# A linear-attention recurrence feeding a bilinear FFN: tokens put in order at y's eviction, and a new written-out order of steps

## The chip, the cores and the metric

The kernel runs on one core of a Trainium2 chip. The metric is the device time in microseconds of one execution, as the median of several runs. A core has five engines that run beside each other, each with a queue of its own that it works off in order: TensorE (PE, matmuls; its weight loads are shown as PEld), VectorE (DVE), ScalarE (ACT), GpSimd (POOL) and SyncE (SP, which here only issues transfers). They wait for each other by semaphores. Transfers (DMA) run beside the engines; they are issued from the queues of SP, POOL and, once, ACT.

## The reference

```python
# q, k, v, alpha: (B, H, S, D) = (4, 8, 768, 48), float32
state = np.zeros((B, H, D, D))
for t in range(S):
    state = alpha[:, :, t, :, None] * state + np.einsum('bhd,bhe->bhde', k[:, :, t], v[:, :, t])
    y[:, :, t] = np.einsum('bhd,bhde->bhe', q[:, :, t], state)

x = y.transpose(0, 2, 1, 3).reshape(B * S, H * D)      # 3072 tokens x 384
a = x @ w_a                                            # 384 -> 1536
b = x @ w_b
out = (a * b) @ w_out                                  # 1536 -> 384
```

A state of 48 x 48 for every head and batch row decays by alpha, takes in k v, and is read by q at each of 768 positions. The result is the input of a feed-forward layer without a nonlinearity other than the product a*b.

## The kernel before

**Chunks.** The recurrence is computed in chunks of positions. A chunk c of six holds 2 of the 4 batch rows (each called u, 0 or 1) and 256 positions, so 512 tokens: c // 2 is the stretch of positions, c % 2 the pair of batch rows. Positions lie in pairs: a partition holds two neighbours, r = 0 and 1. Two halves g of 64 pairs make up the 256 positions of a row u. So the columns of y in PSUM for one u and g are 3 x 128 columns (KT = 3 groups of 128 of the 384 features lie on partitions): for each feature group first the 64 positions with r = 0, then the 64 with r = 1. The tokens of an output block of 128 rows must be in their own order, s by s with r inside.

**Steps.** The whole kernel is one string, PROGRAM, of some 850 short steps, each with the number of its chunk; the loop at L1063 to L1068 emits them in that order, which is so the order of every engine's queue. PROGRAM also names the engine of a step where there is a choice (S = ACT, V = DVE, P = POOL, Y = SP) and the PSUM bank (0 to 7) of a step that writes PSUM. The steps that matter here:

- `ld` (L549) loads a, k, q, v from DRAM on SP or POOL; `W`, `Wo` (L527, L531) load weights on POOL.
- `ln`, `ra`, `E`, `l2`, `l2s`, `R`, `H`, `L`, `lv`, `AQ` prepare the decays: logarithms and exponentials on ACT, running sums on PE (`AQ` L633), products on DVE or POOL (`lv` L652). `mq`, `mk` (L678, DVE) multiply q and k by their decays into QKp.
- `C`, `Ce` (L736, L744) turn QKp with PE for chunks 0 and 1. For chunks 2 to 5 `T u` (L767) turns it by a transposing transfer on SP's queue, which writes kqT.
- `dr`, `dl` (L684, L689) write the decay rows to DRAM and bring them back as bl, on SP's queue.
- `K`, `K2` and `k` (L799, L812, L829, L830) update the state: matmuls, then an addition and a multiplication by bl on DVE.
- `D u h t` (L841) makes the scores from kqT; `M` (L846) masks them on DVE, or `Mc` (L850) copies them on ACT and `Mm` (L854) masks the copy on DVE.
- `SB`, `SA`, `Y` (L865) accumulate y of a row u in two PSUM banks, `X u` (L894 to L902) evicts y as bf16 into xT.
- `a f w bank`, `b f w bank` (L919): three matmuls each for 128 of the 1536 hidden features, over 512 tokens (w is `*`) or the 256 of one row u (w is 0 or 1). `as` (L925) copies a to SBUF on ACT, `pr` (L933) multiplies it by b, straight from PSUM, on DVE and writes prod.
- `o m half bank` (L941): six matmuls for a block m of 128 tokens; `ot` (L956 ACT, L958 DVE) evicts it, `st` (L974) stores it on SP. The last block is done in two halves (`oc` L952, `otc`, `stc`).

**Layout of tokens before.** xT is `[128, KT, B, C]`: feature group, then the 4 half-rows, then 128 columns. X copies y as it stands, so that the columns are in the order r, s. A matmul of a or b reads 512 (or 256) adjacent columns of xT as its rhs. The order is put right at pr: the functions `tokens` and `columns` make its output write every second element, r inside s.

Of the kernel before, what the change touches and what calls it, by code (L numbers as in the profile page):

```python
# [17 lines left out]
0: cm 0; c1; cz 0 b P; ci; ld a 0b Y; c1a; ld a 0a Y; ln 0b; cu; cz 1 b P; fill 7 2; cu2 V; cz 0 q V; cus; ld k 0b Y; ld k 0a Y; B 0b 5; ld q 0b Y; ld v 0 P  # L18
0: ln 0a; ld q 0a Y; E 0b b; E 0b i; mq 0b V; B 0a 0; E 0a i; dk 0 2; E 0a b; ld a 1 P; mk 0b V; C 0 1 5; cs 0 m P; ld k 1 P; ld q 1 P; v 0 S; mk 0a V; cm 1
0: de 0; fill 2 1; mq 0a V; C 0 0 3; Ce 0 1 V; W b 0 256; cz 0 v P; Ce 0 0 V; D 0 1 4; ln 1; ld v 1 P; W a 256 768; K 0 0 6; k 0 0 V; M 0 1; D 0 0 0; SB 0 6  # L20
0: cz 1 q P; B 1a 2; M 0 0; W a 0 256; E 1a i; E 1a b; W b 256 768; mq 1a V; mk 1a V; B 1b 4; dk 1 3; E 1b i; E 1b b; de 1; v 1 S; mq 1b V; mk 1b V; C 1 0 0
0: Y 0; SA 0; Ce 1 0 V; cs 1 m P
1: ld a 0 P; ld a 1 P
0: W a 768 1536; C 1 1 1; X 0 S; c2 P; D 1 0 3; W b 768 1536
1: ld q 0 P
0: Ce 1 1 V; K 1 0 5; k 1 0 V; a 4 0 0
1: ld k 0 P
0: D 1 1 6; SB 1 1
1: ld v 0 P; ld q 1 P
0: Mc 1 0; a 3 0 5; Wo 0 6; a 0 0 3; Mm 1 0 V; Mc 1 1; as 0 0; b 0 0 4  # L30
1: ld k 1 P
0: pr 0 0; b 1 0 6; a 2 0 3; a 1 0 7; a 5 0 4; as 2 0; b 2 0 3; Mm 1 1 V; as 1 0; b 4 0 7; as 5 0; b 5 0 4; pr 2 0; pr 1 0
1: ln 0
0: SA 1; Y 1; Wo 6 12; K 1 1 6; as 3 0; as 4 0; X 1 S
1: ra 0
0: K 0 1 3
1: l2 0 V
0: b 3 0 0; pr 5 0; pr 4 0
1: H 0 V; L 0 V
0: a 2 1 1; a 5 1 2; as 5 1; pr 3 0; a 1 1 7; b 4 1 5; b 5 1 4; as 2 1; k 0 1 V; pr 5 1; a 4 1 2; as 1 1  # L40
1: ln 1
0: b 2 1 0; pr 2 1; a 6 * 3; as 4 1; b 1 1 2
1: l2 1 V
0: pr 4 1; as 6 *
1: H 1 V
0: pr 1 1
1: A2 0 7
0: a 11 * 0; a 7 * 5; a 0 1 4
1: L 1 V
0: k 1 1 V  # L50
1: ra 1
0: as 11 *
1: lv 0 q V; E 0 i
0: as 0 1; b 6 * 0; b 11 * 3; a 8 * 4; pr 6 *; pr 11 *
2: ld a * P
0: b 0 1 1; as 8 *; a 3 1 6
1: E 0 b; lv 0 k V
0: a 10 * 2; pr 0 1
1: mq 0 V; ld v 1 P
0: b 8 * 4  # L60
1: A2 1 7
0: as 10 *; b 10 * 2; pr 8 *
1: E 1 b
0: as 3 1; as 7 *; b 9 * 3; b 3 1 0; b 7 * 1; a 9 * 6
2: ld q * P
1: v 0 S; lv 1 q V; mk 0 V
0: pr 10 *
1: mq 1 V; C 0 1 4
0: as 9 *
1: C 0 0 2  # L70
0: o 0 0 5; pr 7 *
1: dk * 6
2: ld k * P
3: ld v * P
0: cz 1 v P; pr 9 *
1: Ce 0 0 S; E 1 i; de *; lv 1 k P; Ce 0 1 V; D 0 1 1; D 0 0 3
0: pr 3 1
1: Mc 0 0; K2 0 0 7 0
0: o 1 0 6
1: mk 1 V; M 0 1  # L80
0: o 3 0 4; o 1 1 -; ot 1 S; c3 P
3: ld a * P
0: cs 1 0 P; o 3 1 -
1: k 0 0 V; k 0 1 V; Mm 0 0 V; SB 0 1; C 1 0 3; C 1 1 7
0: ot 3 S; o 0 1 -
1: Ce 1 0 V
2: ln *
1: v 1 V; D 1 0 3; Ce 1 1 S; K2 1 1 6 0; Y 0; SA 0
0: ot 0 V
1: k 1 0 V; D 1 1 6  # L90
0: o 2 0 5
1: M 1 0
2: l2 0 V
1: X 0 S; a 3 0 1; Mc 1 1
2: l2s 0 P; l2s 1 P
1: a 2 0 3; a 4 0 4
2: R 0
1: k 1 1 V; as 4 0
2: ra 1
1: as 3 0; b 4 0 7  # L100
0: o 2 1 -
1: as 2 0
0: ot 2 S
1: pr 4 0
2: R 1; lv 1 q P
1: b 3 0 6; b 2 0 7; a 5 0 2; pr 3 0; b 5 0 3; as 5 0; b 1 0 5; a 1 0 1; pr 5 0; pr 2 0; a 7 0 2; as 1 0; pr 1 0
2: AQ 3
1: SB 1 6
2: lv 0 k P
1: a 10 0 5  # L110
2: lv 1 k V; ra 0; ld v * P
1: Mm 1 1 V
2: E 1 b
1: as 10 0; b 10 0 0; pr 10 0
2: mq 1 V; E 1 i
1: as 7 0; b 7 0 1
2: E 0 b; E 0 i
1: a 0 0 5
0: st 3 Y
2: dr  # L120
1: SA 1; Y 1
2: mk 1 V
1: pr 7 0; a 11 0 0; a 6 0 3; b 6 0 2; X 1 S; b 11 0 4; a 2 1 6; as 6 0; a 3 1 7; as 11 0; b 2 1 1; pr 6 0
2: lv 0 q V
1: b 4 1 0; as 2 1
2: T 1
1: pr 11 0
2: dl
0: st 0 Y
1: a 0 1 2; pr 2 1  # L130
2: mq 0 V
1: b 3 1 3; b 0 0 6; as 3 1; as 0 0; b 0 1 7; pr 3 1; a 8 0 1; a 9 0 5
0: st 1 Y
1: b 8 0 3; b 9 0 4; pr 0 0; as 0 1
2: mk 0 V
1: a 4 1 2
3: ln *
1: a 9 1 6; pr 0 1; as 8 0; b 9 1 1
3: ra 1
1: b 10 1 7; pr 8 0; a 10 1 3; as 4 1; as 9 0; as 9 1; a 6 1 6; b 6 1 2; b 11 1 5; pr 4 1; as 10 1; pr 9 0; a 11 1 4; pr 10 1; pr 9 1; as 6 1  # L140
2: v 1 S
1: a 8 1 3; b 8 1 1; a 7 1 6; pr 6 1
3: l2 0 V
1: as 11 1
2: T 0
1: as 8 1; a 5 1 4
3: ra 0
1: as 5 1; a 1 1 2
2: v 0 V
4: ld a * Y  # L150
1: pr 11 1; as 7 1; pr 8 1
2: K2 * * 0 7; D 1 1 3; D 1 0 5
1: as 1 1; b 5 1 2; o 2 0 1
2: k * 0 V
1: pr 5 1
3: v 0 S; v 1 S
1: b 1 1 2
2: Mc 1 0; M 1 1
3: l2s 0 P; l2s 1 P
1: b 7 1 0; o 2 1 -; pr 1 1; o 3 0 4  # L160
2: SB 0 5
1: pr 7 1
3: R 0
2: D 0 0 2
1: ot 2 V
2: Mm 1 0 V
1: o 3 1 -
2: Mc 0 0; SB 1 0; D 0 1 2
3: R 1
1: ot 3 S  # L170
2: SA 0
1: o 0 0 4
0: cs 0 0 P
2: Mc 0 1
4: ln *
3: ld q * Y; ld k * Y
2: k * 1 V
3: AQ 2
2: Y 1; SA 1; Mm 0 1 V; Mm 0 0 V; Y 0; X 0 S
3: E 0 b  # L180
4: l2 0 V
2: X 1 V
1: o 0 1 -
2: b 1 * 6; a 1 * 5
3: E 1 b
4: ld k * Y
3: E 1 i
1: ot 0 S
3: E 0 i
4: l2s 0 P  # L190
2: a 0 * 0; b 0 * 1; as 0 *; as 1 *
3: lv 0 k P; lv 0 q P
2: a 5 * 7
1: st 3 Y
2: a 7 * 4
4: l2s 1 P
2: a 2 * 5
3: lv 1 q V; mq 1 V; lv 1 k V
2: pr 1 *
3: dr  # L200
2: pr 0 *
3: mk 0 V
4: ld q * Y
0: st 2 Y
2: as 5 *; a 6 * 6; b 6 * 2; as 7 *
3: mq 0 V
2: b 9 * 4; b 7 * 0
1: st 2 Y
3: dl
4: R 0  # L210
2: b 5 * 7
1: o 1 0 3
2: a 9 * 1; pr 7 *; as 6 *
3: T 0
2: pr 6 *
4: ra 0
2: pr 5 *; a 11 * 6
3: mk 1 V
2: as 9 *; a 3 * 0
4: lv 0 k V; lv 0 q V; R 1  # L220
2: as 2 *
1: o 1 1 -
2: as 11 *; a 8 * 5; b 11 * 2; a 4 * 7; b 2 * 1
3: T 1
1: ot 1 V
2: pr 9 *; as 8 *; pr 11 *; pr 2 *; b 8 * 3; b 4 * 5; as 4 *
5: ld a * Y
3: K2 * * 4 6
2: pr 8 *; as 3 *; pr 4 *
3: k * 0 V; D 0 0 2; Mc 0 0  # L230
2: b 3 * 1
4: ra 1
2: pr 3 *; b 10 * 5; a 10 * 0
3: D 1 0 1; D 1 1 3
2: as 10 *
3: k * 1 V; Mc 1 1
2: o 0 0 7; o 2 0 0
3: M 1 0
5: ln *
2: pr 10 *  # L240
4: lv 1 q P
3: SB 1 3; D 0 1 1; Mc 0 1
4: lv 1 k P
5: ld q * Y
1: st 0 Y
3: SB 0 5
2: o 2 1 -
3: Mm 1 1 V; Mm 0 0 V; Mm 0 1 V
4: ld v * P
2: ot 2 S; o 0 1 -  # L250
4: AQ 0; E 0 b; E 0 i
3: SA 0; Y 0; SA 1
4: E 1 b
3: Y 1
5: l2s 1 V
4: mq 0 V; mk 0 V
3: X 0 S; X 1 S
2: o 3 0 2; o 3 1 -
4: T 0
3: a 5 * 3  # L260
4: E 1 i; v 0 S
3: a 9 * 0
2: ot 3 S
3: b 5 * 6; a 6 * 5; as 5 *
2: st 2 Y
3: as 9 *
5: ld k * P; l2s 0 P
3: as 6 *
5: ra 1
4: mq 1 V  # L270
2: ot 0 S
3: a 0 * 1
4: mk 1 V
3: a 1 * 2
4: D 0 0 3
5: l2 0 V
1: st 1 Y
4: dr
5: R 0
3: pr 5 *  # L280
4: v 1 S; M 0 0
3: b 1 * 7; as 1 *; a 3 * 5; b 9 * 6; pr 9 *; b 6 * 4; a 2 * 0; pr 6 *
4: T 1
5: lv 0 k P
3: b 0 * 6; as 0 *; as 2 *
4: dl
3: a 8 * 1
5: lv 1 q P
3: b 4 * 0; a 4 * 4; b 2 * 3; pr 1 *; pr 0 *; as 8 *; pr 2 *; as 4 *; pr 4 *; b 3 * 6; b 8 * 2
5: ld v * P; lv 1 k P  # L290
3: a 11 * 1
5: ra 0
3: as 3 *; pr 8 *; as 11 *; a 7 * 0
4: D 1 0 3; K * 0 5
5: lv 0 q P
3: pr 3 *; as 7 *
5: v 1 V
4: k * 0 V
5: R 1
4: D 1 1 6; D 0 1 1; Mc 1 0; Mc 1 1; M 0 1  # L300
2: o 1 0 0; o 1 1 -
3: a 10 * 7; b 11 * 3
4: SB 1 4
2: ot 1 S
3: as 10 *
4: Mm 1 0 V
3: pr 11 *
4: SB 0 1
5: AQ 6; E 0 i; E 0 b; mk 0 V
3: b 10 * 0; b 7 * 3  # L310
4: Mm 1 1 V
5: mq 0 V
3: o 2 0 6; pr 7 *
4: Y 0; SA 0
3: pr 10 *
5: E 1 b
4: X 0 V; Y 1; SA 1
2: st 1 Y
3: o 1 0 3
4: X 1 S  # L320
3: o 2 1 -
5: E 1 i
4: a 7 * 2
5: mq 1 V
4: b 7 * 7; a 6 * 1; as 7 *; as 6 *
3: o 1 1 -
4: b 1 * 5; a 0 * 1; a 1 * 4
5: dr; T 0
2: st 3 Y
4: b 6 * 2  # L330
3: ot 2 V
4: pr 7 *; a 5 * 6
5: mk 1 V
3: ot 1 V
4: pr 6 *
5: v 0 S
4: as 0 *; as 1 *; pr 1 *
2: st 0 Y
5: T 1
4: b 0 * 7; as 5 *; pr 0 *; a 4 * 1; a 3 * 0  # L340
5: K * 0 2; dl
4: as 4 *
5: D 1 0 6; D 0 0 3; M 1 0
4: as 3 *
5: D 1 1 0; Mc 1 1; Mc 0 0; k * 0 V
3: o 3 0 5; o 3 1 -; ot 3 S
4: b 4 * 0; a 2 * 2
5: SB 1 3
4: pr 4 *
5: SB 0 6; D 0 1 0; M 0 1  # L350
3: o 0 0 5; o 0 1 -
5: Mm 1 1 V
4: b 5 * 0
3: ot 0 S
4: b 3 * 1
5: Mm 0 0 V
4: pr 5 *; b 10 * 5; a 11 * 0
5: SA 1; Y 1
4: pr 3 *
5: SA 0  # L360
4: as 11 *
5: X 1 S; Y 0
4: as 2 *
5: X 0 V
4: a 10 * 1
3: st 2 Y
4: b 2 * 4; pr 2 *; b 11 * 7; as 10 *; pr 11 *; pr 10 *
3: st 3 Y
4: a 8 * 3
5: b 9 * 2; a 2 * 0; b 4 * 5; a 4 * 1; b 1 * 6  # L370
4: b 8 * 7; as 8 *
5: as 4 *
4: pr 8 *
5: pr 4 *; a 8 * 4; a 1 * 3; as 2 *; as 8 *; b 8 * 0; a 11 * 5; as 1 *
3: st 0 Y
5: b 2 * 4; pr 1 *; pr 8 *; a 3 * 7; pr 2 *; as 11 *; a 5 * 6
4: o 3 0 0; o 1 0 3
5: b 11 * 1
4: a 9 * 4
5: as 5 *; b 5 * 5; as 3 *; pr 11 *; a 9 * 6; b 3 * 7  # L380
4: as 9 *; b 9 * 1
5: a 10 * 4; pr 5 *
# [716 lines left out]
```

## Time and profile before

| what | value |
|---|---|
| median of 3 runs | 194.33 us (194.84, 193.74, 194.33) |
| span of the profiled execution | 192.04 us (page: 192.0) |
| what lies around the span, against the median | 2.3 us |
| PE busy | 186.8 us, 97% |
| PEld busy (beside PE) | 116.9 us |
| DVE busy | 133.1 us, 69% |
| ACT busy | 106.5 us, 55% |
| POOL busy | 56.9 us, 30% |
| granted clock of PE | 9 (90% or more) in all 40 slices |
| DMA | 29.40 MB, mean 153 GB/s |

Busy times of PE are modelled from pipelined matmuls, whose durations overlap: a matmul of 512 columns is listed with 379 ns on average, though the next starts 216 ns later. The starts of neighbouring instructions tell PE's rate. The rows of a group give: line, engine, operation, output<-inputs, tile shape and form, count; then busy us and mean ns of one; then the idle time of the engine before them and what ended it.

### The profile page before, as it was taken

What the parts mean: (1) busy time and instruction counts of PE and PEld (TensorE: products, weight loads), DVE (VectorE), ACT (ScalarE), POOL (GpSimd) and SP (SyncE); (2) the same over time, 40 slices, a digit from 0 to 9 for tenths busy, and PEclk for the clock granted to TensorE, in tenths of its full rate; (3) what the DMA queues carried; (4) which work ended last, traced back from release to release, by engine and by line L of the source; (5) the groups of instructions that cost most, each with busy time, mean ns of one, the idle gap of its engine ahead of it and who ended that gap; (6) DMA issues with size and microseconds to landing.
All of it is one profiled execution on the core that took longest, in us unless ns stands there. A gap on an engine that the chain in (4) does not pass through costs nothing.

```text
span 192.0 us, 6086 instructions
## 1 busy us (share of the span) xinstructions
PE 186.8 (97%) x2613; PEld 116.9 (61%) x2613; DVE 133.1 (69%) x223; ACT 106.5 (55%) x194; POOL 56.9 (30%) x75
## 2 busy tenths in 40 slices
PE   7999999999999999999999999999999999999992
PEld 3888875677778876645557444656465644545562
DVE  2387698994989888899897956887567446252510
ACT  4448885656779867753487756743572435314211
POOL 8999626752450500640074262000000000000000
PEclk9999999999999999999999999999999999999999
DMA  5999999999969999999999989017641200000422
GB/s 132 274 219 218 251 253 235 244 269 264 251 107 166 165 216 265 248 254 149 233 213 181 156 174 129 3 42 140 146 66 44 85 0 0 0 0 3 164 82 82
DMA packets 62618, 29.40 MB, mean 153 GB/s; under 512 B 53712, under 2 KB 60768, under 8 KB 62592
## 3 DMA queue, kind: packets, MB, share of 16 engines
q0 software_dynamic: 18432, 13.37, 39.6%
q1 hardware_dynamic: 44016, 15.55, 38.1%
q8 instruction: 20, 0.33, 0.7%
q10 hardware_dynamic: 144, 0.10, 0.2%
q14 instruction: 6, 0.05, 0.1%
HBM read 25.98 MB, written 4.74 MB: 160 GB/s over the span
## 4 chain that ended last, share of the span: by engine, by line
PE 91%; DMA 5%; SPq 1%; DVE 1%; issue 1%; ACT 0%; DVEq 0%
PE psum L919 47%; PE psum L941 24%; PE psum L865 7%; PE psum L841 3%; DMA kqT<-QKp 3%; DMA q_t<-in_q_dram 3%; PE psum L736 2%; PE psum L633 1%; PE psum L952 1%; SPq L549 1%; PE psum L799 1%; PE psum L812 1%; PE psum L700 1%; PE psum L591 1%; PE psum L592 1%
## 5 line engine op out<-in xcount | busy, mean ns | idle before, releaser
L919 PE MATMUL psum<-xT,wb_t 128*128 128x512 bf16 (+1 forms) x270 | 56.0, 337 | 0.0
L919 PE MATMUL psum<-xT,wa_t 128*128 128x512 bf16 (+1 forms) x270 | 56.0, 337 | 0.0
L941 PE MATMUL psum<-wo_t,prod 128*128 128x384 bf16 x276 | 49.4, 326 | 0.0
L919 PEld LDWEIGHTS <-wb_t 128*128 128x128 bf16 x270 | 25.9, 98 | 19.9 <-issue 0.5
L919 PEld LDWEIGHTS <-wa_t 128*128 128x128 bf16 x270 | 25.9, 98 | 19.7 <-issue 0.3
L941 PEld LDWEIGHTS <-prod 128*128 128x128 bf16 x276 | 25.9, 98 | 17.6
L956 ACT ACTIVATE ot<-psum 128x384 f32<-128x384 f32 (+1 forms) x16 | 7.7, 482 | 22.7 <-PE psum L941 21.6
L850 ACT ACTIVATE m<-psum 128x1024 bf16<-128x1024 f32 x14 | 14.1, 1023 | 4.6 <-PE psum L841 4.3
L613 POOL TENSOR_TENSOR l<-la 64x384 f32<-64x384 f32 x7 | 7.8, 1108 | 26.6 <-ACT la L556 19.0
L846 DVE TENSOR_TENSOR m<-psum,mask 128x1024 bf16<-128x1024 f32 x10 | 12.1, 1220 | 3.1 <-PE psum L841 3.1
L652 POOL TENSOR_TENSOR q_t<-q_t,ra 128x384 f32<-128x384 f32 x5 | 6.1, 1215 | 22.5 <-ACT ra L645 19.7
L556 ACT ACTIVATE la<-a_t 128x1536 f32<-128x1536 f32 (+2 forms) x9 | 9.5, 1055 | 2.3 <-DMA a_t<-in_alpha_dram 2.2
L678 DVE TENSOR_TENSOR QKp<-q_t,beta 128x768 bf16<-128x768 f32 x10 | 10.0, 995 | 1.0 <-ACT beta L667 1.0
L865 PE MATMUL psum<-m,vx 64*64 64x128 bf16 x576 | 10.5, 217 | 0.0
L900 ACT ACTIVATE xT<-psum 128x768 bf16<-128x768 f32 x9 | 7.2, 816 | 5.7 <-PE psum L865 5.5
L678 DVE TENSOR_TENSOR QKp<-k_t,invb 128x768 bf16<-128x768 f32 x10 | 9.7, 972 | 0.8 <-ACT invb L667 0.8
L854 DVE TENSOR_TENSOR m<-m,mask 128x1024 bf16<-128x1024 bf16 x14 | 9.3, 684 | 1.2 <-ACT m L850 1.2
L958 DVE COPY ot<-psum 128x384 f32<-128x384 f32 (+1 forms) x9 | 4.8, 532 | 7.6 <-PE psum L941 4.7
L865 PEld LDWEIGHTS <-vx 64*64 64x64 bf16 x576 | 9.0, 107 | 0.5 <-issue 0.3
L841 PE MATMUL psum<-kqT 64*64 64x128 bf16 x384 | 9.0, 219 | 0.4 <-DMA kqT<-QKp 0.3
L652 POOL TENSOR_TENSOR k_t<-k_t,a_t 128x384 f32<-128x384 f32 x6 | 7.4, 1228 | 6.1 <-issue 3.3
L549 POOL DMA_DIRECT2D v_t<-in_v_dram x8 | 8.5, 1058 | 0.1
(271 smaller groups left out, 287.9 us busy)
## 6 DMA issues: line engine op xcount, KB each, us to landing
out_dram<-ot SPq DMA_DIRECT2D x23, 192.0 KB, 3.8
q_t<-in_q_dram SPq DMA_DIRECT2D x3, 768.0 KB, 6.5
a_t<-in_alpha_dram POOLq DMA_DIRECT2D x2, 768.0 KB, 15.2
k_t<-in_k_dram POOLq DMA_DIRECT2D x2, 768.0 KB, 12.1
v_t<-in_v_dram POOLq DMA_DIRECT2D x4, 384.0 KB, 7.0
a_t<-in_alpha_dram SPq DMA_DIRECT2D x2, 768.0 KB
k_t<-in_k_dram SPq DMA_DIRECT2D x2, 768.0 KB
a_t<-in_alpha_dram POOLq DMA_DIRECT2D x3, 384.0 KB, 8.5
```

Of the source, the lines that this page charges most:

```text
L549: eng.dma_start(out=t[:, us, hs].rearrange("p b h r d -> p (b h) (r d)"), in_=src[ch.b0 + us.start:ch.b0 + us.stop, hs, ch.s * 2 * C:(ch.s ...
L556: nc.scalar.activation(out=ch.la[:, us, hs].rearrange("p b h r d -> p (b h r d)"), in_=ch.a[:, us, hs].rearrange("p b h r d -> p (b h r d) ...
L613: eng.tensor_add(ch.l2[(1 - g) * HC:(2 - g) * HC, 1], x[:, :, 0, :], x[:, :, 1, :])
L652: eng.tensor_mul(x, x, by)
L678: eng.tensor_mul(QKp[ch.c % 2][:, u, j, :, hs, :D], src[:, u, hs].rearrange("p h r d -> p r h d"), f)
L841: nc.tensor.matmul(s2[g * HC:(g + 1) * HC, r, p, rk, :], lhsT=turned_part(ch, u, 1, rk, 2 * h + p, g, rs), rhs=queriesT(ch, u, 2 * h + p, ...
L846: nc.vector.tensor_mul(m.rearrange("p r a k s -> p (r a) (k s)"), ch.s2[u, h].rearrange("p r a k s -> p (r a) (k s)"), maskn(4))
L850: nc.scalar.activation(out=m.rearrange("p r a k s -> p (r a) (k s)"), in_=ch.s2[u, h].rearrange("p r a k s -> p (r a) (k s)"), func=AF.Copy)
L854: eng.tensor_mul(x, x, maskn(4))
L865: nc.tensor.matmul(y[c * DP:(c + 1) * DP, g, j // 2 * C:(j // 2 + 1) * C], lhsT=lhsT, rhs=rhs, start=(g, c) not in begun, stop=False, skip ...
L919: nc.tensor.matmul(p, lhsT=(wa_t, wb_t)[w][:, kk, f * 128:(f + 1) * 128], rhs=ch.xT[:, kk, us, :], start=(kk == 0), stop=(kk == KT - 1))
L941: nc.tensor.matmul(op, lhsT=ch.prod[:, f, at:at + C], rhs=wo_t[:, f, :], start=(f == 0), stop=(f == NFF - 1))
```

## The change

1. xT becomes `[128, B, KT, C]`: half-row, feature group, column. X takes a second argument, g, and evicts one half: 24 steps of 128 x 384 in place of 12 of 128 x 768. Its output is written with r inside s, so every second element of bf16, and the tokens are in their order from there on.
2. The rhs of a and b is `xT[:, us, kk, :]`: four runs of 128 adjacent columns (two for a half), 384 elements apart.
3. pr writes its product as it comes; `tokens` and `columns` are gone. The eviction uses `evict`, which ot uses too.
4. PROGRAM is another order of the same work. It is the same up to `C 1 0`, but for PSUM banks; from there on steps stand elsewhere, and have other banks, engines or forms. Counted over the kernel: PE has the same 2549 matmuls form by form, DVE 236 instructions in place of 223, ACT 193 (and one DMA issue, as before) in place of 194, POOL 78 and SP 61 as before. The loads on POOL's queue stand in the same order among each other.

In the changed kernel line numbers are 48 smaller up to the eviction (846 to 850); a and b are L861, pr L874, evict L897 and L899.

```diff
-    def evac(ch, u, eng):
+    def evac(ch, u, g, eng):
         if not hasattr(ch, "xT"):
-            ch.xT = wk.tile([128, KT, B, C], BF16, name="xT")
-        o_ = ch.xT[:, :, 2 * u:2 * u + 2, :].rearrange("p a g s -> p g a s")
-        i_ = ch.y[u][0][:, :, :KT * C].rearrange("p g (a s) -> p g a s", a=KT)
-        if eng is nc.scalar:
-            nc.scalar.activation(out=o_, in_=i_, func=AF.Copy)
-        else:
-            eng.tensor_copy(o_, i_)
+            ch.xT = wk.tile([128, B, KT, C], BF16, name="xT")
+        evict(ch.xT[:, 2 * u + g].rearrange("p a (s r) -> p a r s", r=2),
+              ch.y[u][0][:, g, :KT * C].rearrange("p (a r s) -> p a r s", a=KT, r=2), eng)
...
-    def tokens(x, us):
-        return x.rearrange("p (b s r) -> p b r s", s=HC, r=2)[:, us]
-
-    def columns(x, n):
-        return x.rearrange("p (b r s) -> p b r s", r=2, s=HC)
-
...
-            nc.tensor.matmul(p, lhsT=(wa_t, wb_t)[w][:, kk, f * 128:(f + 1) * 128], rhs=ch.xT[:, kk, us, :], start=(kk == 0), stop=(kk == KT - 1))
+            nc.tensor.matmul(p, lhsT=(wa_t, wb_t)[w][:, kk, f * 128:(f + 1) * 128], rhs=ch.xT[:, us, kk, :], start=(kk == 0), stop=(kk == KT - 1))
...
-        o_, a_, b_ = tokens(ch.prod[:, f, :], us), columns(a[:, :n], n), columns(b, n)
-        nc.vector.tensor_mul(o_, a_, b_)
+        nc.vector.tensor_mul(ch.prod[:, f, us.start * C:us.stop * C], a[:, :n], b)
...
-        "X": lambda x, u, e: evac(x, int(u), ENG[e]),
+        "X": lambda x, u, g, e: evac(x, int(u), int(g), ENG[e]),
```

Of PROGRAM, three places that the prediction speaks of. After `C 1 0` in chunk 0:

```diff
-0: W a 768 1536; C 1 1 1; X 0 S; c2 P; D 1 0 3; W b 768 1536
+0: W a 768 1536; C 1 1 2; X 0 0 S; X 0 1 S; c2 P; D 1 0 4; W b 768 1536
...
-0: Ce 1 1 V; K 1 0 5; k 1 0 V; a 4 0 0
+0: Ce 1 1 V; K 1 0 0; k 1 0 V; Mc 1 0; K 1 1 3; D 1 1 6; Mc 1 1; b 1 0 2; a 0 0 0; k 1 1 V; a 1 0 1; SB 1 4
```

Chunk 4's transposing transfers (before: T 0, with D 0 0 as the next step on kqT, then T 1):

```diff
-4: T 0
-3: a 5 * 3
-4: E 1 i; v 0 S
...
-4: D 0 0 3
...
-4: T 1
-5: lv 0 k P
-3: b 0 * 6; as 0 *; as 2 *
-4: dl
+4: v 1 S; mk 0 V; T 0
+3: Y 1; X 1 0 V
...
+4: T 1
+2: ot 0 S
+3: as 9 *; as 8 *
+5: lv 1 q P
+4: dl
+3: b 8 * 0; pr 8 *; as 1 *; b 1 * 2
...
+4: D 1 1 0
...
+4: D 0 1 4; D 0 0 6; v 0 V; M 0 0; M 0 1
```

Chunk 5's:

```diff
-5: dr; T 0
...
-5: mk 1 V
...
-5: T 1
-4: b 0 * 7; as 5 *; pr 0 *; a 4 * 1; a 3 * 0
-5: K * 0 2; dl
-4: as 4 *
-5: D 1 0 6; D 0 0 3; M 1 0
-4: as 3 *
-5: D 1 1 0; Mc 1 1; Mc 0 0; k * 0 V
...
+5: lv 0 q P; mq 0 V; T 0; v 1 V
+4: Y 0; X 0 1 S; Mm 1 0 V; Mm 1 1 V; Y 1
+3: pr 5 *; o 0 0 0; o 2 0 3; o 1 0 5
+5: mq 1 V; mk 1 V; T 1
+4: X 1 1 V; X 0 0 V; X 1 0 S; a 7 * 4
+3: pr 10 *; pr 7 *; o 0 1 -; o 1 1 -; ot 1 V
+5: D 0 0 6
+4: as 7 *
+3: ot 0 S
+5: Mc 0 0; dl; K * 0 2; k * 0 V; D 0 1 0; M 0 1; D 1 1 4; Mc 1 1
+3: o 2 1 -; ot 2 S
+4: a 4 * 2; as 4 *; b 7 * 4; pr 7 *
+3: o 3 0 0
+5: SB 1 2; SB 0 4; D 1 0 6; Mm 0 0 V; M 1 0
```

## Prediction

> **What bounds the kernel now.** I read the page's busy shares first, then the chain that ended last, then the chain's pieces in order of time, then the groups of instructions with shapes kept apart, and last SP's queue around chunk 5.
>
> The page, parts 1, 2 and 4:
>
> ```profile
> span 192.0 us, 6086 instructions
> PE 186.8 (97%) x2613; PEld 116.9 (61%) x2613; DVE 133.1 (69%) x223; ACT 106.5 (55%) x194; POOL 56.9 (30%) x75
> ...
> PE   7999999999999999999999999999999999999992
> ...
> PEclk9999999999999999999999999999999999999999
> ...
> PE 91%; DMA 5%; SPq 1%; DVE 1%; issue 1%; ACT 0%; DVEq 0%
> ```
>
> TensorE is busy in every slice between the first and the last, at the full granted clock. A busy PE need not be PE at its rate, so the chain's pieces decide (start, length, what):
>
> ```profile
> 106.47 4.99 DMA kqT<-QKp
> 111.50 0.42 PE psum L841 x16
> 111.92 9.17 PE psum L919 x42
> ...
> 129.08 1.80 PE psum L865 x120
> ...
> 141.65 0.68 PE psum L841 x46
> ...
> 152.81 11.11 PE psum L919 x51
> ...
> 188.69 0.33 ACT ot L956
> ```
>
> 9.17 us for 42 matmuls of L919 and 11.11 for 51 are 218 ns for 512 columns: they run back to back. In the single instructions the starts lie 216 ns apart at 512 columns, 109 at 256, 163 at 384 (L941), and each change between 128x128 and 64x64 tiles and back costs about 0.3 us. The sum of these over all of PE's instructions is 185.3 us. Outside the first 12 us, where little can be fed to PE, I find only two waits: 0.14 us at 24.4 and 0.36 us at 111.1, the end of the transfer that the first line shows (T of chunk 4, issued at 106.47). The last matmul ends at 188.65; an eviction, a store's issue and its landing fill the rest up to 192.04. So the time is PE's work, plus a start and a tail of a few us each, plus 0.5 us of waits. A change can win no more than these waits if it leaves PE's work alone. It can lose by a slower matmul, or by making PE wait.
>
> The span is 192.04; the median is 194.33, so 2.3 us lie around the span, and I add them at the end. The three runs lie 0.3% to either side of the median; 0.5%, or 0.97 us, is about what a measurement of this kernel can tell from no change.
>
> **The parts of the change, and their cost.** The groups, shapes apart (mean ns of one is after the busy time):
>
> ```profile
> L941 PE MATMUL psum<-wo_t,prod 128*128 128x384 bf16 x276 | 49.4, 326 | 0.0
> L919 PE MATMUL psum<-xT,wa_t 128*128 128x512 bf16 x162 | 41.2, 379 | 0.0
> L865 PE MATMUL psum<-m,vx 64*64 64x128 bf16 x576 | 10.5, 217 | 0.0
> L841 PE MATMUL psum<-kqT 64*64 64x128 bf16 x384 | 9.0, 219 | 0.4 <-DMA kqT<-QKp 0.3
> L900 ACT ACTIVATE xT<-psum 128x768 bf16<-128x768 f32 x9 | 7.2, 816 | 5.7 <-PE psum L865 5.5
> L958 DVE COPY ot<-psum 128x384 f32<-128x384 f32 x8 | 4.4, 554 | 4.7 <-PE psum L941 4.7
> ```
>
> *PE's instructions.* Both kernels have the same matmuls, form by form (540 of a and b, 276 of o, 24 of oc and the rest). Only the order differs, which changes tile sizes 57 times in place of 56: +0.3 us.
>
> *The rhs of a and b.* It was 512 adjacent bf16; now it is four runs of 128, 384 elements apart (two runs at half width). No row has this shape, so I bound it. From below: L841 reads its rhs as two runs of 64, and 46 such matmuls took 0.68 us, 14.8 ns each (four run at once on the quarters of the array); L865 reads one run of 128 from m, and 120 took 1.80 us, 15.0 ns each. Breaks between runs cost nothing there. Below nothing is excluded, since 216 ns is what the contiguous form takes and the columns stay as many. From above: L633, whose rhs takes every second element, starts its 384 columns 183 ns apart where L941 needs 163; 20 ns on each of 540 matmuls would be 10.8 us. The new rhs is of L841's kind, with longer runs; I take 0.
>
> The Trainium skill speaks against this edit: "Advanced Engine Details and Errata", section "Memory Cachelines", asks for at least two hits on a 16-byte line of SBUF for full rate, and under "PSUM Cachelines" says that any non-contiguous access pattern significantly slows matmuls. By its first rule, runs of 256 bytes hit each line eight times and the sum gets 0, as with L841; by the second, read for SBUF too, the sum would end as in the second rival below. The rows of L841 and L865 bear out the first reading.
>
> *The eviction X.* 12 of 768 columns (816 ns on ACT, 952 on DVE) become 24 of 384, written with a stride of two elements. Nearest rows: 384-wide evictions, 492 ns on ACT and 554 on DVE (L958). Strided bf16 writes cost pr about 8% per element against other DVE rows, so 500 to 600 ns is the bound. A pair costs some 0.2 us more than one X did, on both engines together about 2.4 us over the kernel; but the first half is done 0.3 us sooner. Both engines have room (69% and 55% busy), and between SB/SA/Y and the first a of a chunk, matmuls of the chunk before fill PE. On the path: 0.
>
> *pr.* Its write is now contiguous. Before: 54 of about 725 ns and 36 of 441. At the per-element rate of L829 and L846 it would be about 690 and 424: 54 x 35 + 36 x 17 = 2.5 us less on DVE, at best; at worst nothing, if the PSUM operand sets its rate. It is no gain on the path, as PE does not wait for DVE in steady running. DVE altogether: 13 more instructions (more X's halves, 3 more casts of v, one more transposed copy) against the faster pr: 144 to about 150 us in sums of durations, of 192.
>
> *The order.* The start is copied to C 1 0 and so is its cost. Then I walked the queues of PE, DVE, ACT, POOL and SP with the durations of before, step by step, each step starting when its queue, its inputs and its PSUM bank are free. What changes:
> - Chunk 1 half 1: a 4 0 no longer stands between Ce 1 1 and the first D that reads it, so PE waits for DVE's copy, which ends at 18.5: +0.15 us. The wait at 24.4 goes: -0.14.
> - Weights. Loads are in the same order in every queue, so they land as before: W b 256-768 at 20.4, W a 768-1536 at 25.9, W b 768-1536 at 28.8. Their first readers come at 20.8, 26.9 and 29.5. Spare 0.4 to 1.0 us: 0.
> - T of chunk 4 leaves at 105.5 and 111, and is first read at about 120: the 0.36 us wait goes. T of chunk 2 (63.4, read at 71.5) and of chunk 3 (85.3 and 88.9, read at 92.5 and 96.8) have 1 to 2 us to spare, with 4.3 to 6 us from issue to data as in before.
> - Chunk 5 is the narrowest. SP's queue in before (start, length of the issue):
>
> ```profile
> 135.99 1.80 SPq L767 DMA_TRANSPOSE kqT<-QKp  x1
> 137.91 1.64 SPq L689 DMA_DIRECT2D bl<-row  x2
> 140.00 0.36 SPq L974 DMA_DIRECT2D out_dram<-ot  x1
> ```
>
>   The order stays T 1, then dl, which brings the decay rows bl back. Now T 1 can leave when mk 1 is done, at about 131.1, is read at 137.0 by D 1 1, and lands at 135.4 to 137.1 by T's other times. dl follows at 133 to 134.6; in before bl lands 2.1 to 4.1 us after its second issue: 136.4 to 139.7 with the spread of T's own issue. The multiply of k * 0 on DVE comes up at 137.3. Behind it on DVE stand M 0 1 and pr 7 of chunk 4, and SB 0, at 140.8 on PE, waits for the bank that pr 7 frees. Behind bl the chain needs 0.56 (the multiply, as L830's rows) + 1.23 (L846) + 0.72 (L933) = 2.5 us, so bl costs nothing up to 138.3, and at 139.7 it costs 1.4. Most of the interval lies before 138.3; I take 0.1.
> - Elsewhere the spare time is 0.15 to 0.35 us between 20 and 28 us, about 0.5 around 56 to 68 and 86 to 100, and small before AQ at 53 and D 0 1 of chunk 2 at 73.9. I take 0.1 for what falls through. The bound is 0 to 2 us (rival 3).
> - Tail: the last eviction is again ACT's after one store's issue, the last store SP's instead of ACT's: 0, within 0.1.
>
> Sum: 192.04 + 0.3 + 0 (rhs) - 0.36 - 0.14 + 0.15 + 0.1 (bl) + 0.1 (spare times) = 192.2, and with 2.3 around it 194.5. Without the two uncertain waits it is 194.3.
>
> **The rivals.**
> 1. *Slower: bl comes late.* One wait in chunk 5: T 1, dl, k * 0's multiply, M 0 1, pr 7, SB 0. It decides from 138.3 on, and passes 195.3, the bound of the measurable, at 139.3. At 139.7: 194.3 + 1.4 = 195.7. For it: bl lands at 141.1 in before, close behind T. Against it: mk 1 is done 5 us sooner. Measured from T 1's issue, bl in before came 5.1 us later, which gives 136.2 here.
> 2. *Slower: the runs slow the rhs.* 10.8 us at L633's rate, half of it if half of the reads are hit: 200 to 205. For it: L633. Against it: L841.
> 3. *Slower: DVE falls behind.* It has 23.5 us of work between 55 and 75 in place of 20.3. DVE operations beside POOL's take longer in before (lv 1.35 against 0.55 us, mq 1.38 against 1.0): about 0.4 each, and four or five such that meet no spare time give 1.6 to 2 us: 195.9 to 196.3. For it: the spare times are a few tenths. Against it: each stall pushes PE back and so restores spare time for what follows.
> 4. *Faster: ordinary runs of before wait longer for T.* T of chunk 4 took 4.99 us in the profile and cost 0.36; a T that takes 6, as another did, would cost about 1 us more, in before alone, since the new order reads it 9 us later. Then 194.3 - 1.0 = 193.3. For it: PE waits there for nothing else. Against it: the three times lie within 1.1 us of each other, so the runs of before differ by no more in all. A bigger gain would need less PE work, which no part gives.
> 5. *It doesn't do what it says:* pr keeps 725 ns. DVE then has 2.5 us more, hidden: within the forecast.
>
> **How the numbers follow.** Forecast, with 5, at 194.5: 0.60 (194.0 to 195.3). Rival 1: 0.10. Rival 2: 0.06. Rival 3: 0.14. Rival 4: 0.10. The first is within 0.5% of 194.33, the three slower ones make 0.30, the faster 0.10. The range leaves out rival 2, most of rival 4 and what several late steps together could give: 193.5 to 196.8.
>
> **What would show it.** Each step right: L861's 512 columns still start 216 ns apart and 256 columns 109; X rows near 500 (ACT) and 560 ns (DVE); pr rows near 690 and 424 ns; no DMA piece at T of chunk 4 in the chain; PE's last matmul at 188.4 to 189.2; bl of chunk 5 before 138. Wrong: L861 pieces over 220 ns a matmul (rival 2), a DVE piece in the chain between 55 and 100 us (rival 3), a bl or DVE piece at 138 to 142 (rival 1), a PE sum of starts under 185 us.

## The result, and the profile after

The changed kernel takes 202.84 us (median of four runs, 200.43 to 204.84) against 194.06 for the kernel before (four runs): slower. The forecast was 194.5, with a range up to 196.8. The four runs fall into two pairs, 200.43 and 200.99, and 204.69 and 204.84; the ratio to before, 1.034 (95% interval 1.029 to 1.039), and the profile, of the run of 200.99, are of the first pair, which is what this section explains.

Parts 1 and 2 of the page:

```profile
span 199.2 us, 6088 instructions
...
PE 189.0 (95%) x2612; PEld 118.5 (59%) x2613; DVE 137.9 (69%) x236; ACT 102.0 (51%) x193; POOL 57.3 (29%) x75
...
PE   7999999999999999979982999999999999999993
...
PEclk9999999999999999999999799999999999999999
```

PE is idle in the slices near 85 and from 100 to 109, and the granted clock falls behind the second gap. The waits of PE (us in total, times, longest) name both:

```profile
PE psum L585 <- ACT m L802: 4.3, 1, 4.3
...
PE psum L861 <- DVE prod L874: 1.1, 1, 1.1
```

L585 is AQ of chunk 4, which needs the PSUM bank that Mc 0 1 of chunk 3 (L802, ACT) reads. Why was ACT late? ACT's timeline (start, length, instruction, idle time before it):

```profile
99.55 0.59 ACT L867 ACTIVATE as__2094<-psum 128x512 bf16<-128x512 f32 x1
105.56 1.48 ACT L508 ACTIVATE la<-a_t 128x1536 f32<-128x1536 f32 x1 [5.42 <-DMA a_t<-in_alpha_dram]
106.95 1.00 ACT L802 ACTIVATE m<-psum 128x1024 bf16<-128x1024 f32 x1
```

ACT stood at ln * of chunk 5 and waited 5.42 us for chunk 5's alpha; Mc 0 1 was next in its queue. In the kernel before the same ln ran at 99.14 without a wait. SP issued this alpha load 1.0 us later than before (91.25 and 92.27), but POOL's timeline differs by far more. Before (ACT, SP, then POOL):

```profile
99.14 1.48 ACT L556 ACTIVATE la<-a_t 128x1536 f32<-128x1536 f32 x1
```

```profile
91.25 0.96 SPq L549 DMA_DIRECT2D a_t<-in_alpha_dram  x1
```

```profile
97.16 1.00 POOL L652 TENSOR_TENSOR q_t<-q_t,ra 128x384 f32<-128x384 f32 x1 [13.30 <-ACT ra L645]
98.11 1.32 POOL L652 TENSOR_TENSOR k_t<-k_t,a_t 128x384 f32<-128x384 f32 x1
99.37 1.20 POOL L549 DMA_DIRECT2D v_t<-in_v_dram  x1
100.57 1.17 POOL L549 DMA_DIRECT2D k_t<-in_k_dram  x1
```

After (POOL, then SP):

```profile
88.37 1.00 POOL L604 TENSOR_TENSOR q_t<-q_t,ra 128x384 f32<-128x384 f32 x1 [5.34 <-DMA q_t<-in_q_dram]
89.33 1.71 POOL L604 TENSOR_TENSOR k_t<-k_t,a_t 128x384 f32<-128x384 f32 x1
90.98 1.20 POOL L501 DMA_DIRECT2D v_t<-in_v_dram  x1
92.18 1.17 POOL L501 DMA_DIRECT2D k_t<-in_k_dram  x1
```

```profile
86.76 5.42 SPq L719 DMA_TRANSPOSE kqT<-QKp  x2
92.27 1.40 SPq L501 DMA_DIRECT2D a_t<-in_alpha_dram  x1
```

Before, POOL sat 13.30 us on its step lv 1 q, waiting for ra 1 of chunk 4 (ACT), and that wait held back the two loads behind it (v of chunk 4, k of chunk 5) until alpha and q had landed. The new PROGRAM has ra 1 of chunk 4 ahead of chunk 3's transposing transfers. POOL passes lv 1 at 88 to 91 and its loads leave 8.4 us sooner, between the last transposing transfer and the alpha load. In the single packets of the trace, alpha and q of before move 680 to 780 packets of 384 bytes a microsecond from 94 to 98. After the change it is about 330 a microsecond from 97 to 99, while as many packets of the v load pass, and 58 to 150 a microsecond from 99 to 102, while 4 KB packets of the k load pass.

The clock, by stretches (span of time, length, then busy us of PE, PEld, DVE, ACT, POOL with counts, granted clock, DMA share, GB/s):

```profile
104.00:108.00 4.00, 0.00 (x0) 0.00 (x0) 0.01 (x1) 2.40 (x2) 0.00 (x0) 1.00 0.84 195
108.00:110.00 2.00, 1.85 (x64) 1.54 (x67) 2.00 (x4) 1.26 (x4) 1.38 (x1) 0.69 0.04 9
110.00:112.00 2.00, 2.00 (x80) 1.87 (x71) 1.91 (x2) 1.71 (x4) 1.33 (x2) 0.50 0.02 4
112.00:114.00 2.00, 2.00 (x18) 1.21 (x13) 2.00 (x5) 1.23 (x3) 0.70 (x1) 0.95 0.00 0
```

From 108.8 to 112.2 PE runs at half its clock. The account, from PE's starts: 4.5 us lost at AQ, 1.2 us at 86.6 (pr, see e5_ln_later_six_ot), 3.4 us at half clock = 1.7 lost. Together 7.4, against a span 7.0 longer than the 192.2 of the sum; the small waits that the sum had put in (0.15, 0.1 and 0.1) are not among PE's waits.

### The profile page after: what moved, and what is told of

Its sections match the earlier page's. It is cut to its first block, busy times and chain, and to the rows that moved or that the text cites. A ratio compares the mean times of both kernels' runs of the same rounds, so it can differ in the third digit from the quotient of the medians.

```text
span 199.2 us, 6088 instructions
## 1 busy us (share of the span) xinstructions
PE 189.0 (95%) x2612; PEld 118.5 (59%) x2613; DVE 137.9 (69%) x236; ACT 102.0 (51%) x193; POOL 57.3 (29%) x75
## 5 line engine op out<-in xcount | busy, mean ns | idle before, releaser
L861 PE MATMUL psum<-xT,wb_t 128*128 128x512 bf16 (+1 forms) x270 | 55.5, 337 | 1.1 <-DVE prod L874 1.1
L861 PE MATMUL psum<-xT,wa_t 128*128 128x512 bf16 (+1 forms) x270 | 55.8, 337 | 0.0
L882 PE MATMUL psum<-wo_t,prod 128*128 128x384 bf16 x276 | 48.7, 326 | 0.0
L861 PEld LDWEIGHTS <-wb_t 128*128 128x128 bf16 x270 | 25.6, 98 | 22.0 <-issue 1.8
L861 PEld LDWEIGHTS <-wa_t 128*128 128x128 bf16 x270 | 25.9, 98 | 18.6
L565 POOL TENSOR_TENSOR l<-la 64x384 f32<-64x384 f32 x7 | 8.3, 1183 | 41.8 <-PE psum L585 31.8
L802 ACT ACTIVATE m<-psum 128x1024 bf16<-128x1024 f32 x14 | 14.1, 1022 | 6.1 <-PE psum L793 6.0
L897 ACT ACTIVATE xT<-psum 128x384 bf16<-128x384 f32 x13 | 7.2, 597 | 10.5 <-PE psum L817 9.6
L897 ACT ACTIVATE ot<-psum 128x384 f32<-128x384 f32 (+1 forms) x15 | 7.0, 468 | 9.4 <-PE psum L882 8.2
L817 PE MATMUL psum<-m,vx 64*64 64x128 bf16 x576 | 11.3, 232 | 0.1
L630 DVE TENSOR_TENSOR QKp<-k_t,invb 128x768 bf16<-128x768 f32 x10 | 10.7, 1065 | 0.0
L817 PEld LDWEIGHTS <-vx 64*64 64x64 bf16 x576 | 10.2, 117 | 0.6 <-issue 0.3
L899 DVE COPY ot<-psum 128x384 f32<-128x384 f32 x10 | 5.5, 553 | 6.6 <-ACT ot L897 2.7
L899 DVE CAST xT<-psum 128x384 bf16<-128x384 f32 x11 | 6.0, 579 | 3.2 <-PE psum L817 3.2
```

Of the source, the lines that this page charges most:

```text
L630: eng.tensor_mul(QKp[ch.c % 2][:, u, j, :, hs, :D], src[:, u, hs].rearrange("p h r d -> p r h d"), f)
L802: nc.scalar.activation(out=m.rearrange("p r a k s -> p (r a) (k s)"), in_=ch.s2[u, h].rearrange("p r a k s -> p (r a) (k s)"), func=AF.Copy)
L817: nc.tensor.matmul(y[c * DP:(c + 1) * DP, g, j // 2 * C:(j // 2 + 1) * C], lhsT=lhsT, rhs=rhs, start=(g, c) not in begun, stop=False, skip ...
L861: nc.tensor.matmul(p, lhsT=(wa_t, wb_t)[w][:, kk, f * 128:(f + 1) * 128], rhs=ch.xT[:, us, kk, :], start=(kk == 0), stop=(kk == KT - 1))
L882: nc.tensor.matmul(op, lhsT=ch.prod[:, f, at:at + C], rhs=wo_t[:, f, :], start=(f == 0), stop=(f == NFF - 1))
L897: nc.scalar.activation(out=o_, in_=i_, func=AF.Copy)
```

## The experiments

Runs of the kernel before beside each set gave medians of 194.0 to 194.2.

**Is it the layout?** e3_before_order_new_layout keeps the order of before and takes all of the layout.

```diff
 (kernel before, with the new evac, ff and ff_prod)
-X 0 S
+X 0 0 S; X 0 1 S        (all 12 X so, each half on the engine that X had)
```

> The kernel before with the new layout alone: its order of steps is kept, each X is two halves on the same engine, xT is half-row first, a and b read runs of 128, pr writes contiguously. Theory A (the order costs, the layout nothing): starts 216 ns apart at 512 columns, time 193.5 to 195. Theory C (the layout costs): 198 or more.

Measured: 194.05 us (ten runs), ratio 0.9995 (0.998 to 1.001). The layout costs no time here, rhs of separate runs included. The reverse, e4_after_order_old_layout, gives the changed order the old layout:

```diff
 (changed kernel)
-            ch.xT = wk.tile([128, B, KT, C], BF16, name="xT")
+            ch.xT = wk.tile([128, KT, B, C], BF16, name="xT")
...
-        nc.vector.tensor_mul(ch.prod[:, f, us.start * C:us.stop * C], a[:, :n], b)
+        o_, a_, b_ = tokens(ch.prod[:, f, :], us), columns(a[:, :n], n), columns(b, n)
+        nc.vector.tensor_mul(o_, a_, b_)
```

> The changed kernel's order with the old layout: X by halves but written as it stands, a and b read adjacent columns, pr writes every second element. Theory A: the same wait at AQ of chunk 4 and the same fall of the clock, 200 to 205 us, pr back at 725 ns. Theory C: 194 to 196.

Measured: 202.44 us (four runs, 199.56 to 206.89), ratio 1.030 (1.026 to 1.034; of the runs of 199.56 and 200.52), with the same wait:

```profile
PE psum L585 <- ACT m L802: 4.6, 1, 4.6
```

Here SP issued alpha at 91.47, 0.2 us from the 91.25 of the kernel before, and ACT still had to wait for it until after 104. So the order costs, and not by issuing alpha later.

**Which place in the order?** e1_ln_later moves the waiting instruction, e2_pool_loads_after_alpha moves POOL's loads.

```diff
 e1_ln_later
-5: ln *
 3: Mc 0 1; Mm 0 1 V
...
 4: E 1 b
-5: ra 0
+5: ln *; ra 0
```

> The changed kernel with one step moved: ln * of chunk 5 (ACT) stands after E 1 b of chunk 4, just ahead of ra 0 of chunk 5, in place of ahead of Mc 0 1 of chunk 3. Theory A (ACT's queue: ln waits for a late alpha load, Mc 0 1 stands behind it, and AQ on PE waits for the bank that Mc 0 1 reads; then the clock falls): PE's wait of 4.3 us goes, and with it the half clock from 108.9 to 112.1 (1.65 us): span 199.2 - 6.0 = 193.2, time 194 to 196. Theory B (the data of alpha itself is what the chain needs, so that the wait moves to the next reader): 199 to 201. Theory C (the strided rhs or the new X is what costs): no change, 200 to 203.

Measured: runs of 195.71 and 195.98, ratio 1.008 (1.005 to 1.011), and two of 205.22 and 207.40, of which no trace was kept. In the profile (the run of 195.71) the wait at AQ is gone and the clock is 1.000; alpha still lands late, but nothing on the path stands behind it. So the ACT queue was the link between the late alpha and PE.

```diff
 e2_pool_loads_after_alpha   (gate: POOL copies one element of alpha, so it waits for its landing)
 3: SA 0
+5: gate a 0
 4: ld v * P; E 0 i; E 1 i
```

> The changed kernel with POOL made to wait for the alpha load of chunk 5 before it issues v of chunk 4 and k of chunk 5. Theory A1 (alpha landed late because these two loads, issued at 91.0 and 92.2, shared the DMA engines with it): alpha, issued at 92.3, lands by 101.5, about 9 us after its issue as in the kernel before, PE's wait at AQ falls from 4.3 to under 0.5 us, time 194.5 to 196.5; v of chunk 4 then lands near 110 and may make ACT's cast wait 1 to 2 us. Theory A2 (it landed late because SP issued it late, behind the two transposing transfers): alpha lands at 104 or later all the same, time 199 or more.

Measured: 194.88 us (ten runs, 194.6 to 195.8), ratio 1.0047 (1.003 to 1.007). SP issued alpha at 91.56, no earlier than in e4, but POOL's loads left at 98.2, and PE does not wait at AQ. With the loads out of the way alpha is in time: contention, not its issue, made it late. The wait feared for the cast of v did not come.

**The one step.** e7_before_ratio_early moves ra 1 forward in the kernel before; e8_after_ratio_late moves it back in the changed one.

```diff
 e7_before_ratio_early   (kernel before)
 3: T 0
 2: pr 6 *
-4: ra 0
+4: ra 0; ra 1
...
 2: b 3 * 1
-4: ra 1
```

> The kernel before with one step moved: ra 1 of chunk 4 (ACT) stands right behind ra 0, ahead of the transposing transfers of chunk 3, as it roughly does in the changed kernel; nothing else. POOL's lv 1 q and lv 1 k wait for it, and POOL's loads of v (chunk 4) and k (chunk 5) stand behind these. Theory A1 (POOL runs ahead and its loads collide with the alpha load): the loads leave at about 91 in place of 99.4, alpha lands at 103 to 105 in place of 99 or earlier, ln of chunk 5 waits 4 to 5 us on ACT with Mc 0 1 behind it, PE waits 2.5 to 4.5 us near 101, time 197 to 202. Rival (the collision needs the rest of the new order): 194 to 195.

Measured: 206.64 us (four runs, 206.0 to 207.3), ratio 1.065 (1.061 to 1.070): one exponential on ACT, moved, costs 12.5 us. The direction was right, the size above the 197 to 202 expected, and the victim another. POOL, then SP, then PE's wait:

```profile
87.90 1.21 POOL L548 DMA_DIRECT2D v_t<-in_v_dram  x1
89.18 1.17 POOL L548 DMA_DIRECT2D k_t<-in_k_dram  x1
```

```profile
85.24 9.12 SPq L766 DMA_TRANSPOSE kqT<-QKp  x2
94.45 0.53 SPq L548 DMA_DIRECT2D a_t<-in_alpha_dram  x1
```

```profile
PE psum L840 <- DMA kqT<-QKp: 11.4, 1, 11.4
```

The loads left at 87.9, ahead of T 1 (issued 88.84), and it was T 1 that was caught: PE waited 11.4 us for kqT. While both were under way the DMA engines moved 120 GB/s. In the kernel before they moved 170 while its two transposing transfers had them nearly alone, and 244 in the next six microseconds. First before, then e7:

```profile
86.00:92.00 6.00, 6.00 (x33) 3.00 (x31) 6.00 (x10) 1.58 (x3) 0.00 (x0) 1.00 1.10 170
92.00:98.00 6.00, 6.00 (x134) 3.04 (x132) 5.29 (x10) 3.54 (x6) 0.84 (x1) 1.00 1.12 244
```

```profile
96.00:100.00 4.00, 1.24 (x6) 0.39 (x4) 1.80 (x4) 0.85 (x2) 0.00 (x0) 1.00 1.00 120
100.00:104.00 4.00, 0.00 (x0) 0.00 (x0) 0.00 (x0) 0.00 (x0) 0.00 (x0) 0.68 1.56 126
```

```diff
 e8_after_ratio_late   (changed kernel)
-4: ra 1
 2: as 0 *; pr 0 *; b 5 * 0; pr 5 *
...
 3: K2 * * 4 0; dl; T 0; D 0 0 6; Mc 0 0
+4: ra 1
```

> The changed kernel with the one step moved the other way: ra 1 of chunk 4 stands behind the first Mc 0 0 of chunk 3, as in the kernel before. Theory A1: POOL's lv 1 q starts near 95, its loads leave after 97, alpha lands by 101, no wait over 0.5 us at AQ of chunk 4, time 194.3 to 195.5. Rival A2: 199 or more.

Measured: 195.01 us (ten runs, 193.8 to 195.8), ratio 1.0047 (1.002 to 1.007). POOL waits again for ra, its loads leave late, and ln runs without a wait at nearly the time of before:

```profile
94.82 1.00 POOL L604 TENSOR_TENSOR q_t<-q_t,ra 128x384 f32<-128x384 f32 x1 [11.73 <-ACT ra L597]
...
96.71 1.20 POOL L501 DMA_DIRECT2D v_t<-in_v_dram  x1
```

```profile
99.83 1.49 ACT L508 ACTIVATE la<-a_t 128x1536 f32<-128x1536 f32 x1
```

**Two victims, by the order of issue?** If loads ahead of T 1 catch T 1, and loads behind it catch alpha, then the same kernel can be pushed either way.

```diff
 e12_loads_ahead_of_t1   (changed kernel)
-4: lv 1 k P
 3: Mm 1 1 V
...
 5: ld k * P
+4: lv 1 k P
```

> The changed kernel with POOL's lv 1 k of chunk 4 moved behind its two loads, so that v of chunk 4 leaves at about 89.4 in place of 91.0, ahead of chunk 3's T 1 (90.2). Theory E: T 1 is caught, PE waits 7 to 11 us for kqT at chunk 3's D 1, with the half clock after it, 204 to 208 in every run. Rival: 200 to 201, as with the loads behind T 1.

```diff
 e11_loads_after_t0   (changed kernel; gatet: POOL waits for T 0's kqT)
-3: SA 0
+3: SA 0; gatet 0
 4: ld v * P; E 0 i; E 1 i
```

> The changed kernel with POOL made to wait for the landing of chunk 3's T 0 before it issues v of chunk 4 and k of chunk 5. Theory E (two collisions: loads that leave ahead of T 1 stretch T 1 itself, as in e7_before_ratio_early; loads that leave after it stretch the alpha load behind it): the loads leave at 92 to 95, so T 1, issued near 90, is never caught; D of chunk 3 waits under 0.5 us for kqT; alpha still shares with the loads, lands at 100 to 104, PE waits 0 to 4 us at AQ of chunk 4; time 194.5 to 201 and no run over 203. Rival (T 1 is slow in some runs for another reason): runs of 204 to 207 as before.

e12 took 203.99 us (201.02 to 206.59), ratio 1.043 (1.036 to 1.049; of the runs of 201.02 and 203.85), so not all four runs reach the 204 expected. In its profile (span 202.1) v left at 88.70 and T 1 at 89.64, and PE waited for kqT (POOL, SP, then PE's wait):

```profile
88.70 1.21 POOL L501 DMA_DIRECT2D v_t<-in_v_dram  x1
```

```profile
89.64 4.68 SPq L719 DMA_TRANSPOSE kqT<-QKp  x1
```

```profile
PE psum L793 <- DMA kqT<-QKp: 6.9, 1, 6.9
```

In e11 the loads left at 91.83 and 93.03, behind T 1 (90.88), which landed 4.4 us after its issue; the victim was alpha:

```profile
91.83 1.21 POOL L501 DMA_DIRECT2D v_t<-in_v_dram  x1 [0.50 <-issue]
```

```profile
90.88 1.93 SPq L719 DMA_TRANSPOSE kqT<-QKp  x1
```

```profile
PE psum L585 <- ACT m L802: 4.6, 1, 4.6
```

Its runs took 195.3, 200.5, 200.7 and 201.4, the last one profiled; none was over 203, though four runs are few, and the wait is above the 4 us expected. The times overlap (a run of e12 took 201.02), but the two profiles show the two victims as expected. All traces in which the loads leave near T 1 agree: T 1 is caught in the three where v left 0.94 us ahead of it (e5, e7, e12), and not in the five where v left 0.73 to 0.95 us behind it (the changed kernel, e1, e4, e6, e11). In these five v's first packet moves only as T 1's last one is through, within 0.05 us. Whether the changed kernel's own runs of 204.7 and 204.8 are those in which T 1 is caught was not seen in a trace of that kernel (e5_ln_later_six_ot, below, shows it in a near relative).

**The clock.** e6_fill_the_wait gives PE something to do while it waits.

```diff
 e6_fill_the_wait   (changed kernel)
-2: ot 2 V; o 0 0 0
-4: AQ 1; E 0 b
+2: ot 2 V
+0: fill 22 0
+4: AQ 1
+2: o 0 0 0
+4: E 0 b
```

> The changed kernel with 22 idle matmuls of 512 columns (4.75 us; they write a bank that nobody reads) ahead of AQ 1 of chunk 4, and o 0 0 0 of chunk 2 (six matmuls, 1.0 us) moved behind AQ 1. PE so does not idle while Mc 0 1 is late. Theory A with the clock (the wait costs twice: once as idle time, once by the half clock after it): the granted clock is 1.000 in the whole span, PE's rows after 108 run at the full rate, and the span is 199.2 - 1.65 + 1.0 = 198.5, time 200.3; all runs lie within 1 us. Rival (the half clock is not from the idle time): the clock falls all the same, time 201.5 or more.

Measured, with the wait of ACT still 4.8 us: runs of 199.68 and 199.84 (span 197.9 profiled), ratio 1.030 (1.026 to 1.033), and two of 207.8 and 208.8, so not within 1 us of each other as expected. In the profile the clock stays up:

```profile
106.00:108.00 2.00, 2.00 (x20) 0.73 (x19) 0.70 (x2) 1.26 (x2) 0.06 (x1) 1.00 0.16 36
108.00:110.00 2.00, 2.00 (x78) 1.42 (x78) 1.91 (x4) 1.67 (x5) 1.92 (x2) 1.00 0.03 8
```

They are 1.0 us faster than the first pair of the changed kernel, though the edit adds matmuls and pushes 1.0 us of work behind the wait: idle time of PE had been paid a second time in clock.

**The 1.2 us at 86.6.** In the changed kernel DVE waited for a buffer of ot that a store had not left:

```profile
83.54 0.56 DVE L899 COPY ot<-psum 128x384 f32<-128x384 f32 x1 [1.36 <-DMA out_dram<-ot]
```

```diff
 e5_ln_later_six_ot   (e1_ln_later; the same in both places where ot is made)
-ch.ot[m] = wk.tile([128, d_model], F32, name="ot", bufs=4)
+ch.ot[m] = wk.tile([128, d_model], F32, name="ot", bufs=6)
```

> The kernel of e1_ln_later with six buffers for ot in place of four. Theory D (PE's wait of about 1.1 us at 86.5 comes from DVE, whose eviction ot 1 waits at 82 to 83.5 for a buffer that an old store has not left yet, with pr behind it): the wait goes, the transposing transfers of chunk 3 leave 1 to 1.5 us earlier, fast time 195.8 - 1.1 = 194.7. Rival (DVE is simply late there, by its load beside POOL): the wait at 86.5 stays above 0.7 us, time 195.5 to 196.

Measured: six of eleven runs took 194.46 to 195.32, ratio 1.0042 (1.002 to 1.006), against 1.008 for e1; the other five took 204.9 to 206.8, and the profile is of one of these (205.23). Up to 90 us it shows theory D right: DVE's wait is gone, T 0 of chunk 3 leaves at 85.35 in place of 86.76, and PE's gap, now near 90, is 0.45 us. After that it shows T 1, issued at 89.74, caught by the load of v at 88.80:

```profile
PE psum L792 <- DMA kqT<-QKp: 8.8, 1, 8.8
```

So the ten microseconds of these runs are T 1 caught, as far as one profile shows. That in the six others T 1 leaves first was not seen: no trace of them was kept. It is likely from the traces above, and from e1's, where v left 0.74 us behind T 1 in a run of 195.71.

**Is a version faster than both?** Two attempts.

> e8_after_ratio_late with six buffers for ot and ln of chunk 5 behind E 1 b. If the three places found are all that the new order loses: PE's waits after 12 us add to under 1 us, time 193.8 to 194.6, the same as the kernel before (194.1), since PE's own work is 0.3 us more. Rival (more small waits remain, DVE beside POOL near 97 and 117): 194.6 to 195.5.

```diff
 e9_all_three = e8_after_ratio_late
+ six buffers for ot, and ln * of chunk 5 moved as in e1_ln_later
```

Measured: 195.42 us, ratio 1.0066 (1.004 to 1.009). The rival held. What remains are small waits, one of them 1.2 us near 21 us for W b 256-768, which the prediction had put at 0.4 us to spare; it is 0.4 us in e8, 1.3 in e11 and nothing in the changed kernel's profile.

> e3_before_order_new_layout with chunk 0's X 1 on two engines at once (one half on DVE, one on ACT, in place of both on ACT) and six buffers for ot. In e3 PE waits 0.39 and 0.61 us near 24 us for that X, which took 1.05 us on ACT. If halves on two engines are what the new layout is worth, these waits fall to about 0.4 together and the time is 194.05 - 0.6 = 193.5, against 194.15 for the kernel before. Rival (the time is PE's own work and its start, and varies by more): 193.9 to 194.3.

```diff
 e10_layout_two_engines = e3_before_order_new_layout, six buffers for ot
-0: SA 1; Y 1; Wo 6 12; K 1 1 6; as 3 0; as 4 0; X 1 0 S; X 1 1 S
+0: SA 1; Y 1; Wo 6 12; K 1 1 6; as 3 0; as 4 0; X 1 0 V; X 1 1 S
```

Measured: 194.27 us (twelve runs), ratio 1.0013 (0.9997 to 1.0029): no gain. PE's waits, by its starts, are still 0.36 and 0.40, near 25 and 28 us. Nothing tried beats the kernel before; its PE has hardly a wait to give.

## Why the prediction was wrong

**The bound** was read rightly: PE has the same work, and every microsecond lost is a wait or a slow clock.

**The rhs, X, pr.** Right. The starts of a and b lie 216 and 109 ns apart, as before, and e3 is 0.9995 of the kernel before. So rival 2 falls: runs of 256 bytes cost nothing. Of the two readings of the Trainium skill ("Advanced Engine Details and Errata", section "Memory Cachelines") the trace agrees with the one by cachelines. X takes 597 ns on ACT and 579 on DVE: within the bounds of 500 to 600, but on ACT not near the 500 named as a sign. pr takes 681 and 414 ns on average (taken: 690 and 424).

**"Loads are in the same order in every queue, so they land as before."** This is the step that failed. The sentence stands with the weights, and the other loads were priced by the same thought, at nothing. The order of POOL's loads did not change; the time at which POOL reaches them did, by 8.4 us. In the kernel before a wait for ra 1 of chunk 4 held that queue up to 97.16, and I did not list ra 1 among the steps that moved, nor ask what stood behind POOL's wait. e7 and e8 show that this step decides, with 12.5 us in the one kernel and most of the loss in the other (200.7, the mean of the first pair, to 195.0). None of the five rivals spoke of POOL's queue or of two transfers under way together.

**"With 4.3 to 6 us from issue to data as in before"** took the durations of transfers for properties of the transfers. T 1 took 15.0 us beside POOL's loads in e12 and 19.8 in e7; alpha, issued at 92.27, kept ACT waiting to 105.5 in the changed kernel.

**The list of readers was too short.** I walked the weights, T and bl, but not alpha of chunk 5, whose reader ln * stands on ACT ahead of an instruction that PE needs. e1 shows that link.

**No price for idle PE.** The sum charged a wait by its length. The wait of 4.5 us also cost 1.7 us of clock. The Trainium skill has this rule ("TensorE: Matmul & The Clock Gate", section "What's actually happening"): half rate after an idle window of about 3.4 us, full rate after a busy one. The trace agrees: 4.5 us idle, then a clock of 0.50 for 3.4 us; the gap of 1.2 us at 86.6 left it at 1.00.

**The remaining terms.** Chunk 4's wait for T and chunk 5's late bl did not occur (rival 1). Rival 3's waits for DVE did, one of 1.2 us, by a buffer of ot and not by POOL. With ra 1 put back (e8) the rest is 195.0 where the sum gave 194.5. Of the 2.3 us around the span 0.5 was too much: the runs that list their span have 1.7 to 1.9 around it, so the profiled run of before was one of the quicker ones.

## What to carry to other kernels

A wait on an idle engine can be what keeps its transfers apart from others: before moving a step, follow who waits for it, and list every transfer that stands behind that wait, with the time at which it would then leave. A transfer's duration depends on its neighbours: where two could now overlap, price both with the other beside them. And an idle gap on TensorE can be paid again in clock: here those of 4.3 us and more were, unless idle matmuls filled them, and those of about 1 us were not. So one late load can cost more than its delay.

## What the hardware showed that I had not expected

- A transposing transfer slows greatly when POOL's loads were issued 0.94 us ahead of it: issue to landing is 4.4 us in e8 and e11, 6.8 in the changed kernel, 15.0 in e12, and in e7 19.8 on the chain. Meanwhile the DMA engines together moved 117 to 150 GB/s in e12, against 170 in the kernel before, where the transposing transfers had them nearly alone. The single packets take longer too: T 1's of 256 bytes 54 to 65 ns on average in e5, e7 and e12, against 22 in the kernel before, and the 4 KB packets of the k load 390 to 440 ns against 230. So the transfers get in each other's way, and do not only stand in line; by what mechanism no run shows.
- The second collision is milder: plain loads from SP behind POOL's, 271 GB/s in all between 100 and 104 us, but alpha's share falls to a fifth or less for some microseconds. The Trainium skill says that each DMA engine takes turns between the queues of the software and hardware descriptors ("DMA: Bandwidth & Descriptors", section "SWDGE vs HWDGE vs iDMA"); the packet counts agree with turns taken packet by packet: 332 of alpha's against 330 of v's from 97 to 98 us, 58 of alpha's 384 bytes against 60 of k's 4 KB from 100 to 101. No run here tested the rule by itself.
- The half clock lasts 3.41 us in the changed kernel and e11, 6.83 in e4, e5 and e12, and 10.24 in e7: one, two and three times the same length.
- Writing bf16 at a stride of two costs ACT 107 ns on 384 columns (597 against 490 in e4), DVE 29 (579 against 550).
